# Attention and a feed-forward layer on one core: q and k of the first four blocks loaded in 1 KB pieces and turned 64 columns at a time, the two counts spread by TensorE

## The chip, the core and the metric

The kernel runs on one core of a Trainium2 chip. Five engines work in it from queues of their own: TensorE (PE; its weight loads are shown as PEld), VectorE (DVE), ScalarE (ACT), GpSimd (POOL) and SyncE (SP), which issues nearly all transfers. The metric is the device time of one execution in microseconds; lower is better.

## What is computed

Attention over 4 batches, 8 heads, 768 rows and 64 columns a head, with a bias by distance, masked to a local window and a few global keys; then a feed-forward layer on the 3072 x 512 result:

```python
scores = scale * np.matmul(q, k.transpose(0, 1, 3, 2))
is_global = pos[None, :] < int(n_global)
is_local = (rel >= 0) & (rel < int(n_local))
keep = is_global | is_local
dist = np.where(is_global & ~is_local, float(n_local), np.abs(rel).astype(np.float32))
scores = np.where(keep, scores - slopes[:, None, None] * dist, -1000000000.0)
a = softmax(scores)                     # written out in the reference
x = np.matmul(a, v)                     # then the heads side by side: 3072 x 512
h = x @ w_in                            # 512 x 2048
g = h * (1.0 / (1.0 + np.exp(-1.702 * h)))
out = g @ w_out                         # 2048 x 512
```

n_global (8) and n_local (96) arrive as two 64-bit numbers in memory, so the masks can only be made once they are on the chip.

## The kernel before

**Blocks and chunks.** The rows of a batch are cut into 6 blocks of 128. Blocks 0 to 3 of the program are the first blocks of the four batches; they see only their own keys. The other 20 follow batch by batch. Two blocks make a chunk of 256 rows, and the feed-forward layer goes over 12 chunks: `up` (h, L787, and from the fourth chunk L827, a seven-product scheme over tiles pa and pb) and `down` (y, L895). These lines and L536 and L567 to L569, the attention of the later blocks, are nearly all of TensorE's work.

**The first four blocks** (`prep_first`, L408; `first`, L581). SP loads q and k of a block (L397) into the tile raw, 128 rows by 8 heads by 64 columns. TensorE turns each by four transposes of 128 columns, two heads at a time (L422), into the PSUM tile tq. ACT and DVE copy the turned q, each 64 partitions, into QZ, and ACT copies the turned k into KF (L429; the tile is shown as hl, whose memory it uses). QZ has zeros where the other head of the pair would stand (POOL, L414), so that one f32 matmul over 128 rows gives one head's scores. Then come the scores s plus the mask (L604, L605; four heads a step), the largest of each row (DVE, top, L609), its transposition (aux, L612) and copy (mT, L613), the scores once more with queries and keys exchanged (sT, L623 to L625), the exponential (ACT, pt, L636), the product with v (pv, L631), the division (DVE, L665 to L669) and the transposition of x (tx, L689), from which the feed-forward layer starts.

**The masks.** POOL writes positions, DVE makes distances (L301 to L305). The two counts are loaded into all 128 partitions (ci, L244), converted on DVE (`counts`, L307), and then used as a per-partition number for the mask of a block on itself (`own`, L323) and on the block before (`other`, L329). `slopes` (L334) multiplies these by the eight heads' slopes into mm: the part for the block itself in two halves, on DVE (L340) or ACT (L338), and the part for later blocks in one task.

**The weights.** w_in and w_out come as 64-bit floats (ws, L206) and are put together from their words on DVE and ACT (L370 to L378).

**The order** is made at build time by `Work.order` (L104): every task has costs on the engines that can do it, a due time worked back from those who need it, and a correction by its name from the table NUDGE. The planner walks through time and gives each free engine the ready task that is due first. In the first 50 us (WARM) it puts fillers on TensorE where it expects a hole: pairs of 128x512 matmuls on a constant, tile idle, L1060. Each engine then runs its list strictly in order. Fillers and turned tiles share one ring of two PSUM tiles (`r_h`), so a turn waits until the tile that it takes has been copied out.

Of the kernel before, what the change touches and what calls it, by code (L numbers as in the profile page):

```python
# [8 lines left out]
F32 = mybir.dt.float32  # L9
# [3 lines left out]
I32 = mybir.dt.int32  # L13
# [6 lines left out]
P = 128  # L20
# [6 lines left out]

NUDGE = {"T2": -1.5, "down02": 1.4, "down05": -8.2, "down07": -0.8, "down103": 6.7, "down113": -5.5,  # L30
# [4 lines left out]

NG = 8
SKIP = 24
EARLY = 4

FIRST = 4  # L40
SIGN = [{"DVE": 0.62, "ACT": 1.0}]
TURN_X = 4
WARM, GAP = 50.0, 0.5
AHEAD = 24.0
BACKLOG = 3.0
# [42 lines left out]
class Work:  # L88
# [15 lines left out]
    def order(self):  # L104
# [17 lines left out]
                        t.due, moved = due, True  # L122
        for t in self.tasks:
            t.due += NUDGE.get(t.tag, 0.0)
        free = dict.fromkeys(("PE", "DVE", "ACT", "POOL", "SP"), 0.0)
        dma, now, done = 1.5, 0.0, []
        worked, spared = 0.6, 0
# [2 lines left out]
        while len(done) < len(self.tasks) + spared:  # L130
            moved = False
            for e in free:
                if free[e] > now or (e == "SP" and dma > now + BACKLOG):
                    continue
                best = None
                for t, at in ready.items():
                    if e not in t.on or at > now or t.early() > now or (best is not None and t.due >= best.due):
                        continue
                    us = t.on[e]
                    if any(max(free[o], now) + c < now + us for o, c in t.on.items() if o != e):  # L140
                        continue
# [12 lines left out]
                if best is None:  # L154
                    if e != "PE" or now > WARM or now < worked + (GAP if worked > 7.0 else 0.0):
                        continue
                    best = self.spare(spared)
                    b = best.bufs[0]
                    if len(b.ring.taken) >= b.ring.bufs and (b.ring.taken[-b.ring.bufs].left or b.ring.taken[-b.ring.bufs].end > now):
                        continue  # L160
                    b.users, b.left = [best], 1
                    ready[best] = now
                    spared += 1
                t, us = best, best.on[e]
# [45 lines left out]
def kernel(  # L210
# [28 lines left out]


    SC = SX * SX * float(D) ** 0.5
    ci = const.tile([P, 2, 2], I32, name="ci")
    for j, src in enumerate((n_local, n_global)):
        nc.scalar.dma_start(ci[:, j], src.bitcast(I32).rearrange("(o x) -> o x", o=1).broadcast_to([P, 2]))  # L244
    cf = const.tile([P, 2, 2], F32, name="cf")
# [60 lines left out]

    def counts(e):  # L307
        nc.vector.tensor_copy(cf, ci)
        nc.vector.tensor_scalar(cnt, cf[:, :, 0], 0.0, None, ALU.is_lt)
        nc.vector.tensor_add(cnt, cnt, cf[:, :, 1])  # L310
        nc.vector.scalar_tensor_tensor(cnt, cnt, float(2 ** 32), cf[:, :, 0], ALU.mult, ALU.add)

    def covered(e):

# [19 lines left out]
    def slopes(e, js, hs=range(H)):  # L334
        for h in hs:
# [3 lines left out]
            else:  # L339
                nc.vector.tensor_scalar(mm[:, h, js], mk()[:, js], f, None, ALU.mult)  # L340

    wk.tag = "masks"
    m0 = add({"POOL": 2.0}, places, bufs=[ints], want=-9.0)
    m0 = add({"DVE": 1.3}, distances, [m0], [ints, flt, mk], -4.0)
    late = add({"POOL": 1.0}, lambda e: None, [m0], want=0.0)
    m0 = add({"DVE": 0.65}, counts, [m0, late])
    covers = add({"DVE": 1.2}, covered, [m0])
    covers.soon = 300.0
    m1 = add({"DVE": 1.1}, own, [m0], [flt, mk])
# [58 lines left out]
    def prep_first(n):  # L408
# [3 lines left out]
        KF = Buf(r_hl, [P, NU, P], F32, f"KF{n}", lambda t: t.bitcast(F32).rearrange("p (u t) -> p u t", u=NU))  # L412
        d = blk[n] = dict(QZ=QZ, KF=KF, sm=Buf(r_sm, [P, 2 * H], F32, f"sm{n}"))
        zero = add({"POOL": 1.0}, lambda e: [nc.gpsimd.memset(QZ()[D * z:D * z + D, :, 1 - z, :], 0.0) for z in range(2)], bufs=[QZ])  # L414
        ld = load(n, raw, (0, 1))
        turned = []
        for z in range(2):
            tq = Buf(r_h, [P, NU, P], F32, f"tq{n}_{z}")

            def turn(e, z=z, tq=tq):  # L420
                for u in range(NU):
                    nc.tensor.transpose(tq()[:, u], raw()[:, z, 2 * u:2 * u + 2, :].rearrange("p h d -> p (h d)"), ident)  # L422

            turned.append((tq, add({"PE": 4 * TURN}, turn, ld[z:z + 1], [raw, tq])))

        def taken(to, z, part):
            tq, t1 = turned[z]
            return add({"ACT": 0.6, "DVE": 0.7}, lambda e: (
                nc.scalar.mul(to(), tq()[part], SX) if e == "ACT" else nc.vector.tensor_scalar(to(), tq()[part], SX, None, ALU.mult)),  # L429
                [t1], [tq, KF if z else QZ])  # L430

        rows = [slice(D * z, D * z + D) for z in range(2)]
        d["qk_ready"] = [zero, *(taken(lambda z=z: QZ()[rows[z], :, z, :], 0, rows[z]) for z in range(2)), taken(KF, 1, slice(0, P))]

    def own_values(n):

# [82 lines left out]
    def unit(n, u, want_s, want_v):  # L519
# [27 lines left out]
        d.setdefault("S", []).append(t1)  # L547
        ex = []
        for j in range(2):
            t2 = add({"DVE": 0.365}, lambda e, j=j: rows(e, j), [t1, M2], [sp, pr])  # L550
# [30 lines left out]
    def first(n, want):  # L581
# [15 lines left out]
        for f in range(2):  # L597
# [6 lines left out]
                        nc.tensor.matmul(sp()[:, j], qp, kp, start=(z == 0), stop=False, skip_group_check=True)  # L604
                    nc.tensor.matmul(sp()[:, j], id16, mm[:, h, 2], start=False, stop=True, skip_group_check=True)  # L605

            t1 = add({"PE": 4 * (mm_s + MM128)}, scores, [M1[f], *d["qk_ready"]], [sp, *QKs], want + 1.2 * f)
            d.setdefault("S", []).append(t1)
            maxed.append(add({"DVE": 0.61}, lambda e, f=f, sp=sp: nc.vector.tensor_reduce(  # L609
                top[:, n, 4 * f:4 * f + 4], sp(), axis=AX.X, op=ALU.max, negate=True), [t1], [sp]))  # L610
# [660 lines left out]
```

## Time and profile before

| what | value |
|---|---|
| median of 3 runs | 602.29 us (601.71 to 604.09) |
| the profiled execution | 602.48 us |
| its span in the profile | 600.7 us |
| TensorE busy | 587.5 us (98%) |
| DVE, ACT busy | 503.0 us (84%), 471.4 us (78%) |
| granted TensorE clock, mean | 0.997 |

The profile is one execution on the chip. A row of the timeline has the start, the duration, the engine, the line of the program, the operation and its tiles, how many are merged in the row, and in brackets how long the engine was idle ahead of it and what ended that. Matmuls overlap: the duration of one reaches past the start of the next, so what a group costs is the step from its start to the next row's start. A row of the waits has who waited, for whom, the total in us, how often, and the longest.

### The profile page before, as it was taken

Reading aid. Unit: us, or ns where it says so; the run is one execution under the profiler, and the core shown is the slowest. Engines: PE = TensorE matmul, PEld = TensorE weight load, DVE = VectorE, ACT = ScalarE, POOL = GpSimd, SP = SyncE. Lnnn points to the kernel's source line nnn. Section 1 sums busy time; section 2 is a strip of 40 time slices with the busy share of each in tenths; the row PEclk is TensorE's granted clock in tenths of the full one; section 3 lists DMA queues with packets and bytes.
Section 4 is the critical chain, followed back from the end, with each engine's and each line's share of the span. In section 5 each row is a group of like instructions: output and inputs, shape, how many; then the busy total and the mean of one; then the engine's idle time right before and its main releaser. Section 6 shows DMA issues by size and latency. Waiting matters only on the chain.

```text
span 600.7 us, 17037 instructions
## 1 busy us (share of the span) xinstructions
PE 587.5 (98%) x6816; PEld 445.9 (74%) x6816; DVE 503.0 (84%) x1177; ACT 471.4 (78%) x1098; POOL 5.8 (1%) x18
## 2 busy tenths in 40 slices
PE   8989999999999999999999999999999999999996
PEld 5878767777777867777677777777678768867895
DVE  6998999999999999789699789798979978766532
ACT  3878899978768988888698899788999978944432
POOL 3000000000000000000000000000000000000000
PEclk9999999999999999999999999999999999999998
DMA  8998799999976768979996999999989999920001
GB/s 225 310 251 260 227 253 198 191 179 197 212 141 128 156 117 186 196 145 196 216 206 163 226 209 238 197 233 198 236 186 223 224 193 228 234 40 3 36 1 41
DMA packets 268502, 109.58 MB, mean 182 GB/s; under 512 B 249536, under 2 KB 250048, under 8 KB 268416
## 3 DMA queue, kind: packets, MB, share of 16 engines
q1 hardware_dynamic: 267984, 108.30, 86.6%
q8 instruction: 55, 0.90, 0.7%
q14 instruction: 31, 0.25, 0.1%
q10 hardware_dynamic: 432, 0.13, 0.1%
HBM read 57.67 MB, written 6.29 MB: 106 GB/s over the span
## 4 chain that ended last, share of the span: by engine, by line
PE 85%; DMA 7%; ACT 4%; DVE 2%; issue 1%; SPq 1%; POOL 0%; DVEq 0%; ACTq 0%; POOLq 0%
PE y L895 36%; PE pa L827 14%; PE h L787 10%; PE pb L827 10%; PE s L536 5%; DMA pt<-hl 3%; DMA QK<-QK 2%; PE s L604 1%; PE pv L567 1%; PE pv L569 1%; PE pv L568 1%; PE sT L623 1%; PE idle L1060 1%; DMA xT<-x 1%; DMA out_dram<-yo 1%
## 5 line engine op out<-in xcount | busy, mean ns | idle before, releaser
L895 PE MATMUL y<-w,g 128*128 128x512 f16 (+1 forms) x1248 | 266.8, 363 | 0.0
L895 PEld LDWEIGHTS <-g 128*128 128x128 f16 x1248 | 117.9, 98 | 103.3
L827 PEld LDWEIGHTS <-w 128*128 128x128 f16 x1728 | 101.3, 98 | 5.0
L552 ACT ACTIVATE p<-p,NM 128x232 f32<-128x232 f32 x160 | 76.4, 480 | 7.0 <-DVE NM L542 7.0
L827 PEld LDWEIGHTS <-T 128*128 128x128 f16 x1296 | 77.1, 98 | 6.0
L787 PE MATMUL h<-xT,w 128*128 128x256 f16 x576 | 69.4, 273 | 0.3 <-DMA xT<-x 0.2
L542 DVE CUSTOM_DVE_ANT_0 p<-s,mm 128x232 f32<-128x232 f32 x160 | 57.7, 395 | 8.2 <-PE s L536 7.3
L787 PEld LDWEIGHTS <-w 128*128 128x128 f16 x576 | 55.2, 98 | 9.3 <-issue 0.6
L557 DVE TENSOR_TENSOR hl<-p,hl 128x464 f16<-128x464 f32 x80 | 50.9, 636 | 10.2 <-ACT hl L556 10.1
L868 DVE SCALAR_TENSOR_TENSOR g<-t,g 128x512 f16<-128x512 f32 x72 | 49.3, 687 | 11.1 <-ACT g L867 10.9
L867 ACT ACTIVATE g<-t 128x512 f16<-128x512 f32 x72 | 45.0, 628 | 9.5 <-DVE t L860 8.1
L556 ACT CAST hl<-p 128x464 f16<-128x464 f32 x80 | 46.1, 576 | 6.4 <-DMA pt<-hl 4.4
L859 ACT ACTIVATE t<-h 128x512 f32<-128x512 f32 (+1 forms) x72 | 35.9, 515 | 18.2 <-DVE h L835 15.1
L835 DVE TENSOR_TENSOR h<-pb,h 128x256 f32<-128x256 f32 x72 | 29.6, 420 | 23.0 <-PE pb L827 19.6
L827 PE MATMUL pa<-xS,T 128*128 128x128 f16 x648 | 45.0, 219 | 0.0
L860 DVE SCALAR_TENSOR_TENSOR t<-t,h 128x512 f32<-128x512 f32 (+1 forms) x72 | 38.2, 553 | 4.6 <-ACT t L859 4.0
L536 PEld LDWEIGHTS <-QK 128*128 128x128 f16 x640 | 36.5, 98 | 3.7 <-DMA QK<-QK 0.2
L536 PE MATMUL s<-QK 128*128 128x128 f16 x320 | 38.4, 219 | 0.1
L827 PE MATMUL pb<-xS,w 128*128 128x128 f16 x540 | 37.5, 219 | 0.0
L567 PE MATMUL pv<-VR,pt 128*128 128x64 f16 x288 | 34.8, 193 | 2.6 <-DMA pt<-hl 2.6
L827 PE MATMUL pa<-xT,w 128*128 128x128 f16 x540 | 37.0, 219 | 0.0
L569 PE MATMUL pv<-VR,pt 128*128 128x64 f16 x288 | 34.8, 193 | 0.0
(181 smaller groups left out, 1079.9 us busy)
## 6 DMA issues: line engine op xcount, KB each, us to landing
ws<-in_moe_w_in_dram SPq DMA_DIRECT2D x8, 1024.0 KB
ws<-in_moe_w_out_dram SPq DMA_DIRECT2D x8, 1024.0 KB
raw<-in_q_dram SPq DMA_DIRECT2D x24, 256.0 KB
raw<-in_k_dram SPq DMA_DIRECT2D x24, 256.0 KB
out_dram<-yo SPq DMA_DIRECT2D x22, 256.0 KB
QK<-QK SPq DMA_DIRECT2D x40, 128.0 KB
raw<-in_v_dram SPq DMA_DIRECT2D x20, 256.0 KB
ws_00again<-in_moe_w_in_dram SPq DMA_DIRECT2D x8, 512.0 KB
```

Of the source, the lines that this page charges most:

```text
L536: nc.tensor.matmul(sp()[:, j, lo:hi], d["QK"]()[:, 0, h, :], K[:, 1 + z, h, P - (hi - lo):], start=(z == 0), stop=(z == 1), skip_group_che ...
L542: nc.vector.tensor_tensor_reduce(out=pr()[:, j, :], in0=sp()[:, j, :], in1=m, scale=-1.0 / SC, scalar=3.0e38, op0=ALU.add, op1=ALU.min, ac ...
L552: ex.append(add({"ACT": 0.473}, lambda e, j=j: nc.scalar.activation(pr()[:, j, :], pr()[:, j, :], AF.Exp, bias=NM[:, n, hs[j]:hs[j] + 1], ...
L556: t4 = add({"ACT": 0.5}, lambda e: nc.scalar.copy(hl()[:, 0, :, SKIP:], pr()), ex, [pr, hl])
L557: t5 = add({"DVE": 0.55}, lambda e: nc.vector.tensor_sub(hl()[:, 1, :, SKIP:], pr(), hl()[:, 0, :, SKIP:]), [t4], [pr, hl])
L567: nc.tensor.matmul(o, ph, V[:, 0, h], start=(s == 0), stop=False, skip_group_check=True)
L569: nc.tensor.matmul(o, pl, V[:, 0, h], start=False, stop=(s == ns - 1), skip_group_check=True)
L787: nc.tensor.matmul(ph()[:, fi, :], w1(s, cc, z, fi), X[:, y, cc, :], start=(j + cc == 0), stop=(j == 2 and cc == NCC - 1))
L827: nc.tensor.matmul(o()[:, fi], w, x()[:, y * NCC + 2 * k + cc, t], start=(first and fi + j + cc == 0), stop=(last and j + cc == 3), skip_g ...
L867: t4 = add({"ACT": 0.53}, lambda e, g=g, tt=tt: nc.scalar.mul(g()[:, 0], tt(), SG / (SX * SW)), u, [tt, g])
L868: t5 = add({"DVE": 0.61}, lambda e, g=g, tt=tt: nc.vector.scalar_tensor_tensor(g()[:, 1], tt(), SG / (SX * SW), g()[:, 0], ALU.mult, ALU.s ...
L895: nc.tensor.matmul(y(), part(zg, f), w2(s, z, f % 2)[:, m], start=(begin and f + j == 0), stop=(end and j == 2 and f == 2 * len(steps) - 1 ...
```

## The change

**Loads.** `load_pairs` takes the place of `load` for q and k of blocks 0 to 3. A tensor of a block comes in two transfers, one for the even and one for the odd heads. A partition now holds four rows next to each other of one head of each parity, so each piece is 1 KB and not 256 bytes; 32 groups of rows are outermost in the partitions, the four pairs of heads within.

**Turns.** Each of the eight slices of such a tile is 128 partitions by 64 columns. The four of the even heads are transposed into partitions 0 to 63 of tq (L448 of the new program), the four of the odd heads are multiplied by the identity, a plain f32 matmul, into partitions 64 to 127 (L450). The copies out of PSUM (L459) put the rows back into order. k of blocks 0 and 1 is copied out in two halves, and the first half of the scores waits for the first of them alone.

**Counts.** They are loaded into one partition, converted there, spread to 128 partitions by a matmul with a row of ones (L361), and copied out by DVE (L362). The masks for later blocks become four tasks that only ACT may take (before, one task on either).

**The table.** NUDGE has other entries throughout, and the code of a new option (HOLD, empty) is there; a line of the table is shown, since its numbers tell nothing by themselves.

```diff
-NUDGE = {"T2": -1.5, "down02": 1.4, "down05": -8.2, "down07": -0.8, "down103": 6.7, "down113": -5.5,
+NUDGE = {"T0": 7.7, "block0": -8.3, "block3": -0.7, "block6": 0.4, "block7": -0.8, "block9": -8.8, "down03": 4.5,
...
-    ci = const.tile([P, 2, 2], I32, name="ci")
+    ci = const.tile([1, 2, 2], I32, name="ci")
...
-        nc.scalar.dma_start(ci[:, j], src.bitcast(I32).rearrange("(o x) -> o x", o=1).broadcast_to([P, 2]))
+        nc.scalar.dma_start(ci[:, j], src.bitcast(I32).rearrange("(o x) -> o x", o=1))
...
+    m0 = add({"PE": 0.2}, lambda e: nc.tensor.matmul(pc(), row, c1, start=True, stop=True), [m0], [pc], COUNTS)
+    m0 = add({"DVE": 0.15}, lambda e: nc.vector.tensor_copy(cnt, pc()), [m0], [pc], COUNTS)
...
-    M2 = add({"DVE": 2.3, "ACT": 2.6}, lambda e: slopes(e, slice(0, 2)), [m2], [mk])
+    M2 = [add({"ACT": 0.65}, lambda e, f=f: slopes(e, slice(0, 2), range(2 * f, 2 * f + 2)), [m2], [mk]) for f in range(4)]
...
+    def load_pairs(n, raw):
+
+        b, i = place(n)
+        ld = []
+        for z in range(2):
+            src = (q, k)[z][b, :, i * P:(i + 1) * P, :].rearrange("(u e) (j t) d -> e j u (t d)", e=2, t=4)
+            dst = raw()[:, z].rearrange("p (e t) d -> p e (t d)", e=2)
+            ld.append([add({"SP": 0.45}, lambda e, src=src, dst=dst, o=o: nc.sync.dma_start(dst[:, o], src[o]), bufs=[raw]) for o in range(2)])
+        return ld
...
-                for u in range(NU):
-                    nc.tensor.transpose(tq()[:, u], raw()[:, z, 2 * u:2 * u + 2, :].rearrange("p h d -> p (h d)"), ident)
-
-            turned.append((tq, add({"PE": 4 * TURN}, turn, ld[z:z + 1], [raw, tq])))
+                for u in range(4):
+                    nc.tensor.transpose(tq()[0:D, u], raw()[:, z, u, :], ident)
+                for u in range(4):
+                    nc.tensor.matmul(tq()[D:P, u], raw()[:, z, 4 + u, :], ident, start=True, stop=True, skip_group_check=True)
+
+            turned.append((tq, add({"PE": 4 * TURN + 4 * FP128}, turn, ld[z], [raw, tq])))
...
+            src = lambda: tq()[part].rearrange("p t (j u) -> p u j t", u=NU)[:, u]
+            dst = lambda: to().rearrange("p u (j t) -> p u j t", t=4)
...
+        if n < KHALF:
+            k_in = [taken(lambda u=u: KF()[:, u:u + 2], 1, slice(0, P), 0.6, slice(u, u + 2)) for u in (0, 2)]
+        else:
+            k_in = [taken(KF, 1, slice(0, P))] * 2
```

How the lists of the engines change is shown at three places. TensorE, from its first turn on, before (tq is the turned tile, 0 for q and 1 for k, the last number counts tiles; idle are fillers, s the scores):

```order
L422 MATMUL tq_0_140<-ident,raw_107 128x128 x4
L1060 LDWEIGHTS idle
L1060 MATMUL idle_146<-idle 128x512
L1060 LDWEIGHTS idle
L1060 MATMUL idle_146<-idle 128x512
L422 MATMUL tq_1_154<-ident,raw_107 128x128 x4
```

and now:

```order
L448 MATMUL tq_0_156<-ident,raw_95 64x128 x4
L450 MATMUL tq_0_156<-ident,raw_95 64x128 x4
L361 MATMUL pc<-c_68,row 128x2
L448 MATMUL tq_1_170<-ident,raw_95 64x128 x4
L450 MATMUL tq_1_170<-ident,raw_95 64x128 x4
L448 MATMUL tq_0_190<-ident,raw_96 64x128 x4
L450 MATMUL tq_0_190<-ident,raw_96 64x128 x4
L448 MATMUL tq_1_204<-ident,raw_96 64x128 x4
L450 MATMUL tq_1_204<-ident,raw_96 64x128 x4
L640 MATMUL s_0_225<-hl_92,QZ_141 128x128
```

All four turns of blocks 0 and 1 now stand in a row ahead of the first score, with the spread of the counts after the first and no fillers between; before, fillers stood behind each of the first three, and the fourth stood within the scores. Ahead of the first turn are eight filler matmuls in both. In all there are 26 filler matmuls before and 12 now. DVE, ahead of its first copy of q (QZ), before (cf, cnt: the counts):

```order
L305 TENSOR_SCALAR mk<-flt 128x128
L429 TENSOR_SCALAR QZ_120<-tq_0_140 64x4x128
L308 CAST cf<-ci 128x4
L309 TENSOR_SCALAR cnt<-cf 128x2
L310 TENSOR_TENSOR cnt<-cnt,cf 128x2
L311 SCALAR_TENSOR_TENSOR cnt<-cnt,cf 128x2
L324 TENSOR_SCALAR flt<-flt,cnt 128x128
```

and now:

```order
L317 TENSOR_SCALAR mk<-flt 128x128
L320 CAST cf<-ci 1x4
L321 TENSOR_SCALAR c_68<-cf 1x2
L322 TENSOR_TENSOR c_68<-c_68,cf 1x2
L323 SCALAR_TENSOR_TENSOR c_68<-c_68,cf 1x2
L459 TENSOR_SCALAR QZ_141<-tq_0_156 64x4x128
L362 COPY cnt<-pc 128x2
L336 TENSOR_SCALAR flt<-flt,cnt 128x128
```

The counts are converted ahead of the copy of q, and the copy of the spread counts stands behind it, with the masks behind that. SP, its first issues, before (raw are q and k, VF is v, ws the weights):

```order
L397 DMA raw_107<-in_q_dram 128x8x64
L397 DMA raw_107<-in_k_dram 128x8x64
L397 DMA raw_115<-in_q_dram 128x8x64
L397 DMA raw_115<-in_k_dram 128x8x64
L441 DMA VF_102<-in_v_dram 128x8x64
L206 DMA ws_0_166<-in_moe_w_in_dram 128x4x512
```

and now:

```order
L423 DMA raw_95<-in_q_dram 128x1x256 x2
L423 DMA raw_95<-in_k_dram 128x1x256 x2
L423 DMA raw_96<-in_q_dram 128x1x256 x2
L423 DMA raw_96<-in_k_dram 128x1x256 x2
L477 DMA VF_109<-in_v_dram 128x8x64
L215 DMA ws_0_151<-in_moe_w_in_dram 128x4x512
```

The order of what is loaded first is the same; each of the first four is now two issues.

More of the change, by code (lines that the diff above doesn't have):

```diff
@@ L40 @@
 FIRST = 4
+KHALF = 2
 SIGN = [{"DVE": 0.62, "ACT": 1.0}]
 TURN_X = 4
+HOLD = {}
 WARM, GAP = 50.0, 0.5
@@ L124, in order @@
             t.due += NUDGE.get(t.tag, 0.0)
+        held = {}
         free = dict.fromkeys(("PE", "DVE", "ACT", "POOL", "SP"), 0.0)
@@ L163, in order @@
                     spared += 1
+                if e in HOLD and best.due < 1e8:
+                    soon = [at for t, at in ready.items() if e in t.on and now < at <= now + min(HOLD[e], 0.5 * best.on[e]) and
+                            t.due < best.due - 1.0 and t.early() <= at]
+                    if now < held.setdefault((best, e), max(soon, default=0.0)):
+                        continue
                 t, us = best, best.on[e]
@@ L241 @@
     SC = SX * SX * float(D) ** 0.5
-    ci = const.tile([P, 2, 2], I32, name="ci")
+    ci = const.tile([1, 2, 2], I32, name="ci")
     for j, src in enumerate((n_local, n_global)):
-        nc.scalar.dma_start(ci[:, j], src.bitcast(I32).rearrange("(o x) -> o x", o=1).broadcast_to([P, 2]))
-    cf = const.tile([P, 2, 2], F32, name="cf")
+        nc.scalar.dma_start(ci[:, j], src.bitcast(I32).rearrange("(o x) -> o x", o=1))
+    cf = const.tile([1, 2, 2], F32, name="cf")
+    c1 = const.tile([1, 2], F32, name="c1")
+    row = const.tile([1, P], F32, name="row")
+    nc.vector.memset(row, 1.0)
     cnt = const.tile([P, 2], F32, name="cnt")
@@ L308, in counts @@
         nc.vector.tensor_copy(cf, ci)
-        nc.vector.tensor_scalar(cnt, cf[:, :, 0], 0.0, None, ALU.is_lt)
-        nc.vector.tensor_add(cnt, cnt, cf[:, :, 1])
-        nc.vector.scalar_tensor_tensor(cnt, cnt, float(2 ** 32), cf[:, :, 0], ALU.mult, ALU.add)
+        nc.vector.tensor_scalar(c1, cf[:, :, 0], 0.0, None, ALU.is_lt)
+        nc.vector.tensor_add(c1, c1, cf[:, :, 1])
+        nc.vector.scalar_tensor_tensor(c1, c1, float(2 ** 32), cf[:, :, 0], ALU.mult, ALU.add)
     def covered(e):
@@ L340, in slopes @@
                 nc.vector.tensor_scalar(mm[:, h, js], mk()[:, js], f, None, ALU.mult)
+    LATE, COUNTS = 1.2, 0.0
     wk.tag = "masks"
     m0 = add({"POOL": 2.0}, places, bufs=[ints], want=-9.0)
+    late = add({"POOL": LATE}, lambda e: None, [m0], want=-9.0)
     m0 = add({"DVE": 1.3}, distances, [m0], [ints, flt, mk], -4.0)
-    late = add({"POOL": 1.0}, lambda e: None, [m0], want=0.0)
-    m0 = add({"DVE": 0.65}, counts, [m0, late])
+    m0 = add({"DVE": 0.7}, counts, [m0, late], want=COUNTS)
+    pc = Buf(r_pv, [P, 2], F32, "pc")
+    m0 = add({"PE": 0.2}, lambda e: nc.tensor.matmul(pc(), row, c1, start=True, stop=True), [m0], [pc], COUNTS)
+    m0 = add({"DVE": 0.15}, lambda e: nc.vector.tensor_copy(cnt, pc()), [m0], [pc], COUNTS)
     covers = add({"DVE": 1.2}, covered, [m0])
     covers.soon = 300.0
-    m1 = add({"DVE": 1.1}, own, [m0], [flt, mk])
+    m1 = add({"DVE": 1.1}, own, [m0], [flt, mk], COUNTS)
     M1 = [add({"DVE": 0.6, "ACT": 1.0}, lambda e, f=f: slopes(e, slice(2, 3), range(4 * f, 4 * f + 4)), [m1], [mk]) for f in range(2)]
     m2 = add({"DVE": 0.7}, other, [m1], [flt, mk])
-    M2 = add({"DVE": 2.3, "ACT": 2.6}, lambda e: slopes(e, slice(0, 2)), [m2], [mk])
+    M2 = [add({"ACT": 0.65}, lambda e, f=f: slopes(e, slice(0, 2), range(2 * f, 2 * f + 2)), [m2], [mk]) for f in range(4)]
     WT, W_ready = {}, {}
@@ L414, in prep_first @@
         zero = add({"POOL": 1.0}, lambda e: [nc.gpsimd.memset(QZ()[D * z:D * z + D, :, 1 - z, :], 0.0) for z in range(2)], bufs=[QZ])
-        ld = load(n, raw, (0, 1))
+        ld = load_pairs(n, raw)
         turned = []
@@ L420, in turn, with taken @@
             def turn(e, z=z, tq=tq):
-                for u in range(NU):
-                    nc.tensor.transpose(tq()[:, u], raw()[:, z, 2 * u:2 * u + 2, :].rearrange("p h d -> p (h d)"), ident)
-            turned.append((tq, add({"PE": 4 * TURN}, turn, ld[z:z + 1], [raw, tq])))
-        def taken(to, z, part):
+                for u in range(4):
[3 more added lines that the diff above has]
+            turned.append((tq, add({"PE": 4 * TURN + 4 * FP128}, turn, ld[z], [raw, tq])))
+        def taken(to, z, part, us=1.0, u=slice(0, NU)):
             tq, t1 = turned[z]
-            return add({"ACT": 0.6, "DVE": 0.7}, lambda e: (
-                nc.scalar.mul(to(), tq()[part], SX) if e == "ACT" else nc.vector.tensor_scalar(to(), tq()[part], SX, None, ALU.mult)),
+            src = lambda: tq()[part].rearrange("p t (j u) -> p u j t", u=NU)[:, u]
+            dst = lambda: to().rearrange("p u (j t) -> p u j t", t=4)
+            return add({"ACT": 0.6 * us, "DVE": 0.7 * us}, lambda e: (
+                nc.scalar.mul(dst(), src(), SX) if e == "ACT" else nc.vector.tensor_scalar(dst(), src(), SX, None, ALU.mult)),
                 [t1], [tq, KF if z else QZ])
         rows = [slice(D * z, D * z + D) for z in range(2)]
-        d["qk_ready"] = [zero, *(taken(lambda z=z: QZ()[rows[z], :, z, :], 0, rows[z]) for z in range(2)), taken(KF, 1, slice(0, P))]
+        q_in = [zero, *(taken(lambda z=z: QZ()[rows[z], :, z, :], 0, rows[z]) for z in range(2))]
+        if n < KHALF:
+            k_in = [taken(lambda u=u: KF()[:, u:u + 2], 1, slice(0, P), 0.6, slice(u, u + 2)) for u in (0, 2)]
+        else:
+            k_in = [taken(KF, 1, slice(0, P))] * 2
+        d["first_ready"] = [[*q_in, t] for t in k_in]
+        d["qk_ready"] = [*q_in, *dict.fromkeys(k_in)]
     def own_values(n):
@@ L549, in unit @@
         for j in range(2):
-            t2 = add({"DVE": 0.365}, lambda e, j=j: rows(e, j), [t1, M2], [sp, pr])
+            t2 = add({"DVE": 0.365}, lambda e, j=j: rows(e, j), [t1, *M2], [sp, pr])
             checks.append(t2)
@@ L605, in scores @@
                     nc.tensor.matmul(sp()[:, j], id16, mm[:, h, 2], start=False, stop=True, skip_group_check=True)
-            t1 = add({"PE": 4 * (mm_s + MM128)}, scores, [M1[f], *d["qk_ready"]], [sp, *QKs], want + 1.2 * f)
+            t1 = add({"PE": 4 * (mm_s + MM128)}, scores, [M1[f], *(d["first_ready"][f] if n < FIRST else d["qk_ready"])], [sp, *QKs], want + 1.2 * f)
             d.setdefault("S", []).append(t1)
```

9 rows, old and new, of the table NUDGE are left out of this document.

## The prediction

> **What bounds the kernel now.** I read the page first, then TensorE's waits in two stretches, then its timeline up to the place where it stops waiting, and last the ACT and DVE rows that stand against that stretch. From the page, the span, the busy times, TensorE's row of the 40 slices and the chain:
>
> ```profile
> span 600.7 us, 17037 instructions
> PE 587.5 (98%) x6816; PEld 445.9 (74%) x6816; DVE 503.0 (84%) x1177; ACT 471.4 (78%) x1098; POOL 5.8 (1%) x18
> PE   8989999999999999999999999999999999999996
> PE 85%; DMA 7%; ACT 4%; DVE 2%; issue 1%; SPq 1%; POOL 0%; DVEq 0%; ACTq 0%; POOLq 0%
> ```
>
> TensorE is busy 98% of the span and carries 85% of the chain that ends last. Only three slices are below 9, the first, the third and the last. So the time is TensorE's work, plus fillers (matmuls on a constant, tile idle, that the planner puts where it expects a hole in the first 50 us), plus waits, plus the store at the end. The waits, first from 0 to 40 us, then from 45 to 590 us (engine and line, what it waited for, us in total, times, longest):
>
> ```profile
> PE idle L1060 <- ACT hl L429: 1.6, 2, 0.9
> PE idle L1060 <- POOL idle L252: 1.3, 1, 1.3
> PE tx L689 <- DVE x L669: 0.7, 1, 0.7
> PE aux L612 <- DVE top L609: 0.6, 1, 0.6
> PE tq L422 <- DVE QZ L429: 0.6, 1, 0.6
> ...
> PE pv L567 <- DMA pt<-hl: 2.6, 3, 1.1
> PE h L787 <- DMA xT<-x: 0.2, 1, 0.2
> ```
>
> All the waiting that an edit of the start can touch is 4.8 us, 1.3 of it ahead of the first instruction; in the following 545 us there are 2.8 us. The rest is fillers, and they show in TensorE's timeline (start, duration, line, operation, tile, count; the step from one start to the next is what a group costs):
>
> ```profile
> 1.33 3.60 PE L1060 MATMUL idle<-idle 128*128 128x512 bf16 x8 [1.33 <-POOL idle L252]
> 4.75 1.09 PE L422 MATMUL tq<-ident,raw 128*128 128x128 f32 x4
> 5.63 1.06 PE L1060 MATMUL idle<-idle 128*128 128x512 bf16 x2
> 6.83 0.78 PE L422 MATMUL tq<-ident,raw 128*128 128x128 f32 x4
> 8.29 1.02 PE L1060 MATMUL idle<-idle 128*128 128x512 bf16 x4 [0.69 <-ACT hl L429]
> 9.15 0.60 PE L422 MATMUL tq<-ident,raw 128*128 128x128 f32 x4
> 9.58 0.59 PE L1060 MATMUL idle<-idle 128*128 128x512 bf16 x2
> 10.02 0.38 PE L604 MATMUL s<-hl,QZ 128*128 128x128 f32 x2
> ...
> 11.29 0.60 PE L422 MATMUL tq<-ident,raw 128*128 128x128 f32 x4
> 11.73 0.39 PE L604 MATMUL s<-hl,QZ 128*128 128x128 f32 x2
> ...
> 15.67 0.27 PE L612 MATMUL aux<-ident,top 128*8 128x128 f32 x1
> 15.78 0.59 PE L1060 MATMUL idle<-idle 128*128 128x512 bf16 x2
> ...
> 19.37 1.00 PE L631 MATMUL pv<-VF,pt 128*128 128x65 f32 x8
> 20.21 0.59 PE L1060 MATMUL idle<-idle 128*128 128x512 bf16 x2
> ...
> 24.59 0.59 PE L1060 MATMUL idle<-idle 128*128 128x512 bf16 x2
> 25.02 1.00 PE L631 MATMUL pv<-VF,pt 128*128 128x65 f32 x8
> ...
> 27.14 0.59 PE L1060 MATMUL idle<-idle 128*128 128x512 bf16 x2
> 28.45 0.66 PE L689 MATMUL tx<-ident,x 128*128 128x128 f32 x4 [0.72 <-DVE x L669]
> ...
> 39.23 1.47 PE L787 MATMUL h<-xT,w 128*128 128x256 f16 x12
> 40.53 0.39 PE L604 MATMUL s<-hl,QZ 128*128 128x128 f32 x2
> ```
>
> Three readings. The array starts slow: eight fillers take 3.42 us (1.33 to 4.75), 0.43 each, and four take 0.86 at 8.29, 0.215 each; the four transposes at 6.83 lie between the two speeds, so until roughly 7 us everything costs double. Four transposes cost 0.88 cold (4.75 to 5.63) and 0.44 warm (11.29 to 11.73). And TensorE does not stop for the loads: the first turn begins as the eight fillers end, and the later ones wait for a PSUM tile to be copied out or for their place in the order. From 39.23 on nothing but the 2.8 us above holds it. So the question is how much TensorE time lies ahead of an equal amount of work.
>
> **The loads.** Each q or k of blocks 0 to 3 goes from one transfer with 256-byte pieces to two with 1 KB pieces. All of q of block 0 has landed by 4.75 in the kernel before, with the slower pieces, and the fillers last to 4.75 in both orders; the gain there is nothing, and the loads of blocks 2 and 3 are not waited for by TensorE in the rows above. I price this part at 0. What follows these on SP (v, the weights) moves by less than a transfer, and no weight is waited for at the start.
>
> **The turns.** This is what the change adds. A turn was four transposes; now it is four transposes into 64 partitions and four f32 matmuls with the identity into the other 64. An f32 matmul in a row of its own kind: four of pv take 19.37 to 20.21, so 0.21 each; the scores, f32 and bf16 in pairs, take 15.67 - 11.73 = 3.94 for twelve pairs, so 0.33 a pair at most. I take 0.21, since the turns too stand in a row of their kind. A turn becomes 0.44 + 0.84 = 1.28, and eight of them add 6.7 us of TensorE work. At 0.33 each the addition would be 10.6, which is 3.9 worse; below 0.21 I see no row.
>
> The Trainium skill, TensorEngine Tiling (Array Packing), section Key Properties, says that changing the tiling mode drains TensorE and that tiles of one mode run independently. No row before shows a tile of 64 columns. By a drain the sum would be the slow rival below, by independent tiles the fast one; the sum itself takes neither.
>
> **The start, step by step.** The rows of ACT and DVE that stand against it:
>
> ```profile
> 7.64 0.60 ACT L429 ACTIVATE hl<-tq 128x512 f32<-128x512 f32 x1 [1.18 <-PE tq L422]
> 15.98 0.26 ACT L613 CAST mT<-aux 8x128 bf16<-8x128 f32 x1 [3.45 <-PE aux L612]
> L832 ACT COPY h<-pb 128x256 f32<-128x256 f32 x36 | 13.3, 370 | 8.1 <-DVE h L835 4.6 <-PE pb L827 3.2
> 6.50 0.69 DVE L429 TENSOR_SCALAR QZ<-tq 64x512 f32<-64x512 f32 x1 [2.57 <-ACT QZ L429]
> 7.22 0.17 DVE L308 CAST cf<-ci 128x4 f32<-128x4 int32 x1
> 8.02 0.29 DVE L324 TENSOR_SCALAR flt<-flt,cnt 128x128 f32<-128x128 f32 x1
> 9.92 0.63 DVE L340 TENSOR_SCALAR mm<-mk 128x128 bf16<-128x128 f32 x4
> ```
>
> Eight fillers to 4.75 as before. Turn of q of block 0, cold: 0.88 and four matmuls at double price, 4 x 0.42, to 7.3. The spread of the counts, one matmul of two columns, about 0.1. Turn of k, warm, 1.28, to 8.7. Then a wait: the next turn takes the PSUM tile of k, which ACT now copies out in two halves. A copy of 128x256 is 0.37, so 0.74 in place of the 0.69 at 8.29; to 9.4. Two turns of block 1, 2.56, to 12.0. Sixteen scores, 10.02 to 15.67 less the turn within, 5.21, to 17.2. The kernel before is at 15.67 here, so the start loses 1.5 us.
>
> Do the masks arrive by 12.0? The spread must be copied by DVE behind its half of q: 7.3 + 0.6 (ACT's half of q, by the row of hl) + 0.69 (DVE's) + 0.2 for the copy (0.17 at L308) = 8.8. From L324 to the end of L340 it is 8.02 to 10.55, 2.5, so 11.3: in time by 0.7 us. If the counts land late, the matmul that spreads them holds TensorE, with the turn of k behind it; they were there at 7.2 before, when they came as 128 pieces, so the cost lies between 0 and 0.7 and I take 0, as they are now one piece. The other masks' eight multiplies move to ACT, at most 8 x 0.37 = 3.0 us; ACT sat idle for 3.45 us ahead of 15.98, and the cast behind them is wanted at 17.3, so that is free. Without that hole it would delay the cast and with it the first sT by up to 3 us.
>
> From aux to the values of block 1 it was 15.67 to 25.02, 9.35; of the three pairs of fillers there one goes (0.43): 8.92, to 26.1. Then the values of block 1 (25.02 to 27.14 less a turn of x of 0.44: 1.68), two turns of x (0.88) and three turns of q and k (3.84), to 32.5. The turn of k of block 2 now lies where TensorE waited for x of block 1 (27.14 to 28.45), so that wait is covered, and so is the one for hl, with another turn. Scores of block 2, half of 5.21, then 48 matmuls of h at 1.30 for twelve, 5.2, to 40.3; aux 0.1 and the last turn 1.28, to 41.7.
>
> The kernel before has done the same when the 24 matmuls of h that it lacks at 39.23 are added: 41.8. So nearly the whole addition is paid by fillers and waits whose place it takes. Counted the other way, 6.7 us of turns and 0.8 for the cold matmuls come in; 14 fillers go (2 x 0.43 + 12 x 0.215 = 3.4), the waits of 0.7, 0.9, 0.6 and 0.6 go, and 0.3 of cold transposes: +1.0. The timetable has no small waits between engines and is some tenths too kind. I take +0.5, between the two. From there on the work is the same, and the order behind it is new in detail. I leave its 2.8 us of waits and the store as they are.
>
> The profiled execution took 602.48 (span 600.7 and 1.8 around it), beside a median of 602.29 (601.71 to 604.09). Plus 0.5 on the median: **602.8 us**.
>
> **Rivals.** *A drain at each switch (slower).* Each turn goes from the whole array to the half and back, 16 switches in all. The four transposes at 9.15 end 0.60 after they began, and the next instruction starts at 9.58, 0.17 before that end; if that pipeline must run empty at each switch, and the 0.155 us in which the next weights are loaded shows too,
>
> ```profile
> L422 PEld LDWEIGHTS tq<-ident,raw 128*128 128x128 f32 x32 | 3.9, 155 | 2.7 <-PE idle L1060 1.0 <-DVE QZ L429 0.8 <-POOL QZ L414 0.7
> ```
>
> it is 16 x 0.17 = 2.7 to 16 x 0.325 = 5.2 us, so 605.5 to 608.0. It decides from 0.16 per switch. Against it: between full-array turns and f32 scores (11.29, then 11.73) nothing is lost. The page of the skill named above states the drain. Chance 0.14.
>
> *More waits for the transposing transfers (slower).* The new order moves the issues on SP throughout; three waits cost 2.6 us now. Twice as many would give 605.4, a little more than that 606. For it: these waits lie scattered, so they depend on the order; against it: DVE has eight multiplies fewer to do early, so what it prepares for later is rather sooner than before. Chance 0.10.
>
> *The two halves of a turn run side by side, and the late waits go (faster).* Four transposes under four matmuls would save 8 x 0.44 = 3.5 us: 599.3; without the late waits 596.5. Against it: no rows before overlap two matmuls' streams. Chance 0.12.
>
> *The change moves nothing* is within my own forecast, since the loads were not waited for. My forecast, within 3 us of 602.3, has 0.64.
>
> **The numbers.** About 0.5%, 3 us, is what a measurement of this kernel tells from no change: faster means under 599.3, slower over 605.3. Faster 0.12; within 0.64; slower 0.24. Late waits may go entirely (-2.8) or double (+2.8), the f32 price adds up to 3.9 and small waits up to 1: the likeliest case by itself holds 600 to 606. With the better part of the drain and the edge of the fast case the range is 599.5 to 607.0.
>
> **What would show it.** Right: L450 at about 0.21 us a matmul; the scores of block 0 start near 12 us, later than 10.02; aux near 17.2; few waits between 13 and 40 us; the last turn ends near 41.7 to 42.2; 12 fillers. Wrong: gaps of 0.15 us or more at each switch between L448 and L450 (drain), starts of L450 under L448 (side by side), a wait of TensorE for the masks at 12 us, or more than 5 us of waits behind 45 us.

## The result and the profile after

The changed kernel took 606.37 us, median of 8 runs (605.53 to 608.34), the kernel before 601.99 us, median of 8 (600.45 to 604.09). The ratio is 1.0072, with a 95% interval of 1.0055 to 1.0090: 4.4 us slower. The profiled execution of the changed kernel is the slowest of its eight, 608.34 us with a span of 606.6, so a difference between the two traces (5.9 us) is larger than that of the medians.

The page of the changed kernel, span, busy times, TensorE's slices and the chain:

```profile
span 606.6 us, 17163 instructions
PE 594.8 (98%) x6867; PEld 452.1 (75%) x6868; DVE 503.3 (83%) x1174; ACT 473.8 (78%) x1105; POOL 5.8 (1%) x18
PE   8999999999999999999999999999999999999995
PE 79%; DMA 7%; ACT 6%; DVE 4%; issue 2%; POOL 0%; SPq 0%; DVEq 0%; ACTq 0%; POOLq 0%
```

The slice below 9 at the start, the third, is gone: TensorE is busy 594.8 us and not 587.5. It does not wait more, it has more to do. Its waits, from 0 to 45 us and then from 45 to 596 us (engine and line, what it waited for, us in total, times, longest):

```profile
PE idle L1096 <- POOL idle L264: 1.3, 1, 1.3
PE tq L448 <- ACT hl L459: 0.7, 1, 0.7
PE tq L448 <- ACT QZ L459: 0.5, 1, 0.5
...
PE pv L603 <- DMA pt<-hl: 1.6, 4, 0.5
PE pa L863 <- ACT h L879: 0.7, 1, 0.7
PE pv L603 <- DMA VR<-VG: 0.3, 1, 0.3
PE pb L863 <- DVE h L871: 0.2, 1, 0.2
```

At the start 2.5 us of waits where there were 4.8, later 2.8 us as before. So the late waits are not the cause. TensorE's timeline over the first four turns (start, duration, line, operation, tile, count; a f32 matmul shows as two records, so four of them are x8):

```profile
4.72 1.06 PE L448 MATMUL tq<-ident,raw 128*64 128x128 f32 x4
...
7.12 0.38 PE L361 MATMUL pc<-c,row 1*128 1x2 f32 x2
7.43 0.63 PE L448 MATMUL tq<-ident,raw 128*64 128x128 f32 x4
...
9.82 0.63 PE L448 MATMUL tq<-ident,raw 128*64 128x128 f32 x4 [0.75 <-ACT hl L459]
...
11.39 0.63 PE L448 MATMUL tq<-ident,raw 128*64 128x128 f32 x4
11.95 1.09 PE L450 MATMUL tq<-ident,raw 128*64 128x128 f32 x8
12.97 0.49 PE L640 MATMUL s<-hl,QZ 128*128 128x128 f32 x2
```

Take the fourth turn. Its four transposes hold the array from 11.39 to 11.95, 0.56 us, where four whole-array ones took 0.44; its eight matmul records from 11.95 to 12.97, 1.02 us, where eight steps of 0.11 would be 0.88. Together 1.58. So about 0.13 us is lost at each change between transposes and matmuls of half the columns, in either direction, on top of the work. No L450 record starts under L448: nothing runs side by side here. The rest of the start, to the last turn:

```profile
27.74 0.60 PE L448 MATMUL tq<-ident,raw 128*64 128x128 f32 x4
28.27 1.09 PE L450 MATMUL tq<-ident,raw 128*64 128x128 f32 x8
29.29 0.66 PE L725 MATMUL tx<-ident,x 128*128 128x128 f32 x4
...
32.20 0.63 PE L448 MATMUL tq<-ident,raw 128*64 128x128 f32 x4 [0.52 <-ACT QZ L459]
...
34.80 1.09 PE L450 MATMUL tq<-ident,raw 128*64 128x128 f32 x8
...
43.76 0.27 PE L648 MATMUL aux<-ident,top 128*8 128x128 f32 x1
43.87 0.60 PE L448 MATMUL tq<-ident,raw 128*64 128x128 f32 x4
44.40 1.09 PE L450 MATMUL tq<-ident,raw 128*64 128x128 f32 x8
```

The last turn ends at 44.40 + 1.02 = 45.4; the forecast had 41.7. The delay stays. The first score of the later blocks, in the view of that line alone (duration in ns, then the first and the last start in us), before and after:

```profile
L536 PE MATMUL s<-QKover,QK x16: 209/209/209, 79.7 to 91.6; 128*128 128x104 f16 x16
```

```profile
L572 PE MATMUL s<-QKover,QK x16: 209/209/209, 84.8 to 95.4; 128*128 128x104 f16 x16
```

5.1 us later. By then the new order has done 1.3 us more of other work: turns, fillers and the spread of the counts left out, six more matmuls of y stand ahead of this place in it, at 0.216 us each. So the start costs 3.8 us of the 4.4.

### The profile page after: what moved, and what is told of

Same layout as the page of the kernel before. It is cut to its first block, busy times and chain, and to the rows that moved or that the text cites. A ratio compares the mean times of both kernels' runs of the same rounds, so it can differ in the third digit from the quotient of the medians.

```text
span 606.6 us, 17163 instructions
## 1 busy us (share of the span) xinstructions
PE 594.8 (98%) x6867; PEld 452.1 (75%) x6868; DVE 503.3 (83%) x1174; ACT 473.8 (78%) x1105; POOL 5.8 (1%) x18
## 4 chain that ended last, share of the span: by engine, by line
PE 79%; DMA 7%; ACT 6%; DVE 4%; issue 2%; POOL 0%; SPq 0%; DVEq 0%; ACTq 0%; POOLq 0%
PE y L931 33%; PE pa L863 12%; PE h L823 10%; PE pb L863 9%; PE s L572 4%; DMA pt<-hl 3%; DMA ws_11again<-in_moe_w_out_dram 2%; ACT p L588 2%; PE s L640 2%; PE tq L450 1%; PE pv L603 1%; PE pv L605 1%; PE pv L604 1%; PE sT L659 1%; DMA raw<-in_k_dram 1%
```

## The experiments

**Theory A**, from the trace: the turns are added TensorE work at 1.55 to 1.58 us each, of which 0.26 is lost at two changes of form; covered fillers and waits pay only part. **Rival B**: the new table and what it does to the waits later. **Rival C**: the counts and masks. **Rival D**: the 1 KB pieces pay part of the price. Times are medians; the ratio is to the kernel before on the same chip, with its 95% interval; the last column is the start of the first score of the later blocks in the profiled execution, where the order is that of the kernel it was made from.

| kernel | us | ratio | that start |
|---|---|---|---|
| before | 601.99 | 1 | 79.7 |
| changed | 606.37 | 1.0072 (1.0055 to 1.0090) | 84.8 |
| before with the half turns | 611.85 | 1.0153 (1.0128 to 1.0178) | 87.3 |
| changed, slices alternating | 613.13 | 1.0160 (1.0132 to 1.0188) | 91.1 |
| changed, matmuls only | 605.85 | 1.0060 (1.0037 to 1.0084) | 83.6 |
| changed, matmuls side by side | 603.57 | 1.0020 (0.9999 to 1.0041) | 80.6 |
| changed, whole turns, 256-byte pieces | 601.29 | 0.9981 (0.9959 to 1.0002) | 78.8 |
| changed, whole turns, 1 KB pieces (values mixed up) | 602.08 | 0.9991 (0.9972 to 1.0010) | 79.4 |
| changed, old counts | 607.16 | 1.0069 (1.0043 to 1.0095) | 83.9 |
| changed, old table | 613.95 | 1.0184 (1.0158 to 1.0209) | other order |
| before, new table | 609.95 | 1.0106 (1.0076 to 1.0135) | other order |
| whole turns, replanned | 603.38 | 1.0008 (0.9994 to 1.0022) | other order |
| whole turns, old table | 607.67 | 1.0078 (1.0056 to 1.0100) | other order |
| whole turns, late ones replanned | 602.55 | 0.9996 (0.9980 to 1.0011) | other order |

**The turns alone, in the kernel before.**

```diff
                 for u in range(4):
-                    nc.tensor.transpose(tq()[:, u], raw()[:, z, 2 * u:2 * u + 2, :].rearrange("p h d -> p (h d)"), ident)
+                    nc.tensor.transpose(tq()[0:D, u], raw()[:, z, 2 * u, :], ident)
+                for u in range(4):
+                    nc.tensor.matmul(tq()[D:P, u], raw()[:, z, 2 * u + 1, :], ident, start=True, stop=True, skip_group_check=True)
```

> The kernel before, with nothing but its eight turns changed: the even heads are transposed into partitions 0 to 63, then the odd heads multiplied by the identity into 64 to 127; loads, counts, table and the order of all work stay, and with it the 26 fillers. Theory A (the time added is TensorE work of the turn: four f32 matmuls of 0.22 us and two switches between the tile shapes at 0.13 us): a turn goes from 0.44 to 1.58 us, eight add 9.1, of which the wait for x (0.7) and part of the waits for copies are covered: 609.5 to 611.5 us, plainly more than the changed kernel, which pays part with 14 fillers fewer. Rival B (the new table and what it does to later waits and the end costs the time, the turns are hidden): under 604.

611.85, 8.9 us over the kernel before: 0.35 above theory A's range of 609.5 to 611.5, and far from rival B's 604. The first score of the later blocks starts 7.5 us later (87.3 for 79.7). Rival B has no part in it: order and table are the old ones.

**The slices alternating.** One loop over u with a transpose and then a matmul, in the changed kernel.

> The changed kernel with the eight slices of a turn taken alternately, transpose, matmul, transpose, matmul, in place of four and four: eight switches of kind in a turn and not two, the same work. Theory A with a price per switch of 0.13 us: 6 x 0.13 x 8 = 6.2 us more, 612.6. If only entering and leaving the 64-column form costs, and not the change from transpose to matmul: no change, 606.4. If the two halves run side by side when neighbours differ (the fast rival of the prediction): four transposes under four matmuls, 3.5 us less, 603.

613.13, 6.8 over the changed kernel. Its timeline, one turn in the warm stretch (L449 is the matmul here):

```profile
11.34 0.30 PE L448 MATMUL tq<-ident,raw 128*64 128x128 f32 x1 [0.75 <-ACT hl L458]
11.57 0.43 PE L449 MATMUL tq<-ident,raw 128*64 128x128 f32 x2
11.94 0.30 PE L448 MATMUL tq<-ident,raw 128*64 128x128 f32 x1
...
13.71 0.30 PE L448 MATMUL tq<-ident,raw 128*64 128x128 f32 x1
```

A pair takes 0.59 (11.34 to 11.94; four of them to 13.71), where its three steps of 0.11 would be 0.33: 0.26 for two changes. The later blocks' first score, in the view of that line, starts 6.3 us behind the 84.8 of the changed kernel:

```profile
L571 PE MATMUL s<-QKover,QK x16: 209/209/209, 91.1 to 101.7; 128*128 128x104 f16 x16
```

48 more changes for 6.3 us: 0.13 each. That is the price, and the whole program's time shows it.

**Matmuls only.** `transpose` becomes `matmul` in the first of the two loops.

> The changed kernel with the four transposes of a turn replaced by f32 matmuls with the identity too, so all eight slices are plain matmuls. The matmuls cost 4 x 0.11 x 8 = 3.5 us more. If a switch costs because the column tile changes (0 to 63, then 64 to 127): the full 3.5 us, 609.9. If it costs because a transpose gives way to a matmul, 0.13 us or more a turn comes back: 607.5 to 608.9. Under rival B (turns hidden) nothing moves: 606.4.

605.85, no dearer than the changed kernel although a turn has sixteen records of matmuls and not twelve: below all that was expected but the reading by which turns are hidden, which the two runs above exclude. The timeline shows why (L448 writes partitions 0 to 63, L450 64 to 127):

```profile
26.52 0.76 PE L448 MATMUL tq<-ident,raw 128*64 128x128 f32 x5
27.02 0.32 PE L450 MATMUL tq<-ident,raw 128*64 128x128 f32 x1
27.12 0.27 PE L448 MATMUL tq<-ident,raw 128*64 128x128 f32 x1
27.18 0.27 PE L450 MATMUL tq<-ident,raw 128*64 128x128 f32 x1
...
27.40 0.71 PE L450 MATMUL tq<-ident,raw 128*64 128x128 f32 x5
28.04 0.66 PE L725 MATMUL tx<-ident,x 128*128 128x128 f32 x4
```

With no transpose between them, records of the two column halves start 0.055 apart. The first L450 starts ahead of the last three L448, though it stands behind all eight in the order. The turn is 1.52 us (26.52 to 28.04).

**Side by side.** The same matmuls, the halves in turn within one loop (L449 is the second half here).

> The changed kernel with all eight slices of a turn as f32 matmuls, even and odd heads alternately (order of all else the same). In the run with matmuls only, the records of the two column halves lie over each other at 0.055 us, but only for three matmul instructions in eight, since four and four stand in a row. If neighbours in different column halves run side by side: a turn is eight steps of 0.11 and about 0.25 for entering and leaving, 1.1 in place of 1.58 us; eight save 3.8: 602.6 (601 to 604). If the overlap there is not real time saved: 16 x 0.11 + 0.25 = 2.0 a turn, 3.4 us more: 609.8.

```profile
24.97 0.22 PE L661 MATMUL sT<-mT,id 128*128 128x128 bf16 x1
25.12 0.32 PE L448 MATMUL tq<-ident,raw 128*64 128x128 f32 x1
25.12 0.33 PE L449 MATMUL tq<-ident,raw 128*64 128x128 f32 x1
25.28 0.27 PE L448 MATMUL tq<-ident,raw 128*64 128x128 f32 x1
25.29 0.27 PE L449 MATMUL tq<-ident,raw 128*64 128x128 f32 x1
25.39 0.27 PE L448 MATMUL tq<-ident,raw 128*64 128x128 f32 x1
...
26.14 0.66 PE L725 MATMUL tx<-ident,x 128*128 128x128 f32 x4
```

Both halves start together, eight steps of 0.11, and the turn is 1.02 us (25.12 to 26.14). About 0.1 more is lost ahead of it: L661, a matmul over the whole array, steps 0.15 here (24.97 to 25.12), and 0.06 where another matmul over the whole array follows. So a turn costs 1.1 us in this order and about 1.6 with matmuls in groups, where the same 0.1 is lost ahead of it (1.52 and 0.1). This also shows that the loss is not one of transposes alone: it comes between matmuls over the whole array and matmuls into half of the columns as well. The first score of the later blocks starts at 80.6, 4.2 earlier than in the changed kernel, and the median is 2.8 lower. So the fast rival's mechanism exists, but only between matmuls. The Trainium skill, TensorEngine Tiling (Array Packing), section Key Properties, has both rules: a change of tiling mode drains TensorE, and tiles of one mode run independently. The runs agree with both; if what is lost at a change is that drain, its price here is 0.13 us. The same page, section Gotcha 2: Feature Incompatibilities, says that column tiling excludes transposing f32. That would put the two drains of a turn at the two ends of its four matmuls, and the step from aux to the transposes (43.76 to 43.87, nothing lost) agrees; no run here shows the mode itself.

**Whole turns again, with the order of the changed kernel.** Table, tasks and the planner's costs stay, so fillers and order stay.

```diff
-            src = (q, k)[z][b, :, i * P:(i + 1) * P, :].rearrange("(u e) (j t) d -> e j u (t d)", e=2, t=4)
...
+            src = (q, k)[z][b, :, i * P:(i + 1) * P, :].rearrange("h p d -> p h d")
...
+                for u in range(NU):
+                    nc.tensor.transpose(tq()[:, u], raw()[:, z, 2 * u:2 * u + 2, :].rearrange("p h d -> p (h d)"), ident)
```

> The changed kernel with its own table, costs and tasks, so that the order stays, but each turn is again four transposes over the whole array, and q and k come again in 256-byte pieces (still two transfers a tensor), which that turn needs. Theory A (the turns are what the change costs): eight times 1.58 - 0.44 = 9.1 us less TensorE work, of which the waits that the long turns covered come back, at most the 3.5 us of the kernel before: 597.5 to 601 us, under both kernels. Rival C (something else of the change holds the start, the counts or the halves of k): 604 or more. Rival D (the 1 KB pieces pay part of the price, so losing them costs): 601 to 604.

> As the run with whole turns, but with the loads in 1 KB pieces; a turn then transposes the wrong pairs of slices, so the values are mixed up, and only the time is read. Theory A (loads priced at nothing): the same time as with 256-byte pieces within 1 us, and the first turn starts near 4.7 us in both. Rival D: 1 to 3 us faster than with 256-byte pieces, and TensorE waits for raw there and not here.

601.29 and 602.08, intervals that overlap. The first is 5.1 us under the changed kernel, the second 4.3; theory A's range ended at 601, so they lie 0.3 and 1.1 above it. The first score of the later blocks starts 6.0 us earlier (78.8 for 84.8). The 1 KB pieces gain nothing that can be measured, where rival D had 1 to 3 us: it falls. The second run also keeps the copies that put the rows back into order, so these are not the cost either. And the counts, the masks and the halves of k are kept in both, where rival C had 604 or more. What comes back of the 9.1 us are waits, in the first of the two from 0 to 45 us:

```profile
PE tq L448 <- ACT QZ L459: 1.3, 1, 1.3
...
PE tq L448 <- ACT hl L459: 0.7, 1, 0.7
PE pv L667 <- ACT pt L672: 0.6, 1, 0.6
PE s L641 <- DVE mm L352: 0.3, 1, 0.3
```

and, behind the first of these, a slower array (timeline, then the granted clock in the row of that stretch, the last but two of its columns):

```profile
28.11 1.09 PE L448 MATMUL tq<-ident,raw 128*128 128x128 f32 x4 [1.33 <-ACT QZ L459]
28.99 1.06 PE L725 MATMUL tx<-ident,x 128*128 128x128 f32 x4
29.85 1.06 PE L448 MATMUL tq<-ident,raw 128*128 128x128 f32 x4
```

```profile
28.00:31.00 3.00, 2.89 (x14) 2.89 (x15) 3.00 (x6) 2.95 (x5) 0.00 (x0) 0.53 1.04 403
```

Twelve transposes take 0.22 each, not 0.11: 1.3 us more.

**Old counts.**

> The changed kernel with the counts as before: loaded to 128 partitions, converted there, no matmul that spreads them (DVE still copies them once). Theory A: the spread costs 0.3 us of TensorE, 606.1 within 1 us. Rival C (the spread delays the masks or holds TensorE): 1 to 3 us less, 603.4 to 605.4.

607.16, where theory A had 606.1 within 1 us, just missed, and rival C 603.4 to 605.4: rival C falls. The start gains 0.9 us in the trace (83.9 for 84.8), which the median does not show; 0.6 of it is the first turn, ahead of the counts, which took 1.80 us and not 2.40.

**The tables exchanged.**

> The changed kernel with the table of the kernel before. Rival B (the new table costs the time): 602 to 604 us. Theory A (the turns cost it at the start): the table moves the late waits only, 606.4 with 2 us to either side.

> The kernel before with the table of the changed kernel, nothing else. With the old table the changed kernel took 614, 7.5 us more. Reading 1 (each table only fits the order for which it was made): the kernel before loses too, 604 to 610. Reading 2 (the new table is better in itself, and hides part of the price of the turns in the changed kernel): 596 to 601, which would mean that the turns cost more than the 4.4 us between the two kernels.

613.95 and 609.95: each program loses some 7 us with the other's table (7.6 and 7.2 by the medians). For the first, theory A had 606.4 within 2 us and rival B 602 to 604, and both missed; the second is in the range of reading 1. Rival B falls in the form in which it stood. The new table is no loss for the changed program; of these two, each fits its own order better. In the changed kernel with the old table the waits behind 45 us are (the largest three)

```profile
PE pv L602 <- DMA pt<-hl: 3.9, 6, 1.3
PE pa L862 <- ACT h L867: 1.4, 2, 0.7
PE s L571 <- DMA QKover<-QKover: 1.1, 1, 1.1
```

6.4 us in these three alone, where all of them were 2.8. In the kernel before with the new table they lie at the start too:

```profile
PE tq L423 <- DVE t L798: 2.3, 1, 2.3
...
PE tq L423 <- ACT QZ L430: 1.3, 1, 1.3
PE tq L423 <- DMA raw<-in_k_dram: 1.0, 1, 1.0
```

**A better version?** Three kernels with whole turns, in which the planner knows their real price (for all turns, with the old table, or for the last four only):

> As the run with whole turns (256-byte pieces), but the planner is told 0.44 us a turn and not 1.3, so that it orders anew: 18 fillers and not 12, in the place where TensorE waited 1.33 us for the copy of q at 28 us and its clock fell. If fillers there are worth their place: 1 to 2 us less, 599.5 to 600.5. If the table fits only the order for which it was made: 603 to 609, as in the run with the old table.

> As the replanned run, with the old table: the new counts, masks and halves of k with old loads, turns and table. If these parts are worth something by themselves: 600 to 602. If the old table fits only the old order: 604 to 610.

> As the run with whole turns, the planner told 0.44 us for the turns of blocks 2 and 3 only, so the first four turns keep their order. Between the run with whole turns, 601.3, and the replanned one; the wait of 1.33 us at 28 us is to be gone or filled.

603.38, 607.67 and 602.55. Fillers with a new order did not pay: the replanned kernel is 2.1 us behind the one that was not replanned (the intervals of their ratios overlap), at the low end of what a misfit table would give, and the old table is a misfit to this order too. What the fillers alone are worth was not tried. In the last of the three the wait of 1.33 us has become others of the same kind (1.30, 1.15 and 1.15 us). No kernel here has an interval that lies below 1. The lowest, whole turns at 601.29 with 256-byte pieces, keeps of the change the counts, the masks, the halves of k and the order, and its interval reaches 1.0002.

## Why the forecast held in part

The forecast was 602.8 with a range of 599.5 to 607.0. The time lies in the range, but not in the case called likeliest: it is 4.4 us slower, and that case ended at 3. It is inside because the range had been widened at its upper end for a part of the drain.

**What failed: "A turn becomes 0.44 + 0.84 = 1.28".** The matmuls cost what was said (0.88 for four, against 0.84), with some luck: the 0.21 was read from pv, whose matmuls take 65 columns and not 128, and happen to cost nearly the same. What was missing is the 0.26 us of two changes of form: a warm turn is 1.55 to 1.58. The loss stood in the prediction as a rival, the drain, with a chance of 0.14, set against the row in which transposes and f32 scores follow each other without loss. That row was for the whole array on both sides and said nothing on half of it. The rival "decides from 0.16 per switch", and the price is 0.13: alone it would have left the time within 3 us, with the forecast's own 0.5. It took the small waits too.

**The timetable of the start.** Predicted and measured ends of its steps, in us:

| step | predicted | measured |
|---|---|---|
| first turn ends | 7.3 | 7.1 |
| spread of the counts | 7.4 | 7.4 |
| second turn ends | 8.7 | 9.0 |
| wait for k's copy ends | 9.4 | 9.8 |
| first score | 12.0 | 13.0 |
| aux | 17.2 | 18.3 |
| values of block 1, or the turn now ahead of them | 26.1 | 27.7 |
| three turns more | 32.5 | 35.8 |
| last turn ends | 41.7 | 45.4 |

Each turn's end is the start of the next row, or the last L450 with its 1.02. Of the 3.7 us, seven warm turns hold 2.0 (10.95 for 8.96) and the cold one gives back 0.15. The rest is what "no small waits between engines" left out: 0.5 for ACT's copy of q at 32.20, 0.2 for the spread (0.31 for 0.1), 0.5 between aux and the next turn, and 0.6 in scores, values and turns of x, whose first instruction behind a change starts late. The forecast allowed up to 1 for these; they are 1.8.

**What was right.** The loads are worth nothing, by the pair of runs with whole turns. The masks were in time: no wait for them at 13 us. 12 fillers remain in the order, and the early waits fell from 4.8 to 2.5. The late waits stayed at 2.8. That fillers and waits pay for the turns that take their place holds for about half of the price, not for nearly all of it: the same turns cost 8.9 us in the kernel before, where nothing was taken out for them, and 4.4 here.

**What stays open.** The start holds 3.8 of the 4.4 us. In the profiled pair another 2.1 lies behind it: 1.3 between the first and the last scores of the later blocks, with equal waits of TensorE, and the rest behind TensorE's last matmul, in the last store. The medians leave 0.6 for it, and runs of one kernel lie 2.8 apart (605.53 to 608.34), so it can be chance; it wasn't tried by itself.

## What to carry to other kernels

Changing between f32 matmuls into half of the columns and transposes, or matmuls over the whole array, had a price of about 0.13 us at each crossing here, so it is the crossings that are to be counted, not only the instructions. If a tile must be turned by halves, matmuls of neighbouring halves in alternation cost less than transposes and matmuls in groups (about 1.1 for 1.58 us a turn), and four transposes over the whole array cost less than either (0.44). Wider packets were worth nothing here, where TensorE wasn't waiting for the load, and either table of nudges cost about 7 us under the order for which it was not made.

## What the runs showed that was not expected

- Two f32 matmuls into different column halves start within 0.01 us of each other (25.12 and 25.12, 25.28 and 25.29), and steps of the pair are 0.11 us as for one. TensorE also starts a later instruction of the free half ahead of up to three earlier ones of the busy half.
- Behind a single wait of 1.33 us, in the first run with whole turns, the granted clock was 0.53 over the next 3 us; waits of 0.75 and 0.52 us (before 9.82 and 32.20 in the changed kernel) left the steps as they were. The length of the wait alone does not decide: in the second run with whole turns a wait of 1.34 us was followed by a turn at full speed (28.58 to 29.07), and the clock fell from 29 us on (0.66, then 0.50 up to 32 us); in the kernel with the late turns replanned a wait of 1.30 us (before 15.26) left it at 1.00 for the next 3 us.
- When the array leaves its slow first stretch varies: in the first whole-turn run the turn at 4.51 took 0.53, in the second, at 4.71, 0.89, with the same eight fillers ahead. These 0.2 and 0.36 are most of the 0.6 us between their starts (78.8 and 79.4). The granted clock reads 1.00 in these first microseconds, so it does not show this slowness.
